# Step 0's second product by seven products on all rows, and step 1's outer convolution blocks by ScalarE taps and accumulating DMAs

## The chip, the core and the metric

The kernel runs on one core of a Trainium2 chip. The metric is device time in microseconds (us). Five engines work side by side, each through its own list of instructions in order: TensorE (PE, matmuls), VectorE (DVE), ScalarE (ACT), GpSimd (POOL) and SyncE (SP). SP and POOL issue DMAs, which sixteen DMA engines carry out; an engine whose next instruction waits for a semaphore holds everything behind it.

## The reference

```python
w = softmax(weight, axis=-1)                  # (8 heads, 7 taps)
x_pad = zeros of 6 rows ahead of x            # x: (8, 4096, 192) float32
out[b, s, h, g] = sum_k w[h, k] * x_pad[b, s + k, h, g]     # 24 columns to a head
h = out.reshape(32768, 192) @ w_in            # w_in: (192, 2048)
g = h / (1 + exp(-1.702 * h))                 # quick gelu
y = g @ w_out                                 # w_out: (2048, 192)
```

A causal convolution of seven taps along the sequence, one set of taps per head, then a two-layer network with the quick gelu between. All of it is float32; `w_in` and `w_out` arrive as 64-bit floats and are rounded to float32 in the kernel.

## The kernel before

The 32,768 tokens are taken in 32 steps (`big` from 0 to 31), each of 512 tokens from each half of the batch. A step has four parts. `transpose_x` (VectorE) turns the tokens of `xin` so that channels lie on partitions, into `xt`, in three blocks `c` of 64 channels by two. The convolution makes `conv_t` out of `xt`. The first product (`hidden`) makes `g`, the gelu of `conv_t` times `w_in_s`. The second (`second`) multiplies `g` by `w_out_s` and by sums of its blocks, the forms in `w_form`, and the result is turned back on VectorE (`turn`) and stored by SP (`store`).

From step 1 on both products use schemes with fewer block products than blocks, in return for sums of blocks. Step 0 differs, since the sums of the weights are not made yet: its first product is done plainly (`plain`), while VectorE and ScalarE round the weights piece by piece (`split`, `rounds`, `round_w_out`), and its second product, `second_first`, uses seven block products in place of eight (matrices in two by two blocks) on half of the 2048 rows of `w_out`, and plain products on the other half. In the code `first` and `other` are the two halves. A `go` of one step is three matmuls for 32 of 96 output columns each (`L802`) and one matmul of a list laid aside (`side`, `L808`), so that four 32-column matmuls fill the array. The lists have 45 such groups. Differences of blocks of `g` (`t1`, `t2`, and `b12`, `b21`, `b22` in place; 128x2048 each) and of `w_out` (`s1` to `s4`; 128x384 each) are made on VectorE in between.

While step 0's second product runs, four other things are prepared.

- **The convolution of step 1** (`prepare(1)`): for blocks 2, 0 and 1, the first tap on ScalarE (`L494`) and six `scalar_tensor_tensor` on VectorE (`L496`) into `conv_t`. Then `SUMS_C` on VectorE (`L391`, `L393`), and `cross`, DMAs on SP (`L532`) that copy `conv_t` over to the other half of the partitions, two short ones for `V1` and then the long ones.
- **The convolution of step 2** has block 1 on VectorE and blocks 0 and 2 as taps: `prepare_taps(2)` puts fourteen calls of `tap` into the list `ready`, and `next_tap` issues the next. A tap is a ScalarE multiplication (`L507`) into a scratch place (`tap_home`). For block 2 POOL adds it on (`L509`). For block 0 the seven taps are added by six accumulating DMAs of POOL's queue (`L521`) in the order of `TREE`: (1,2), (3,4), (5,6), (0,1), (3,5), (0,3). In the first steps the scratch places are rows of `g` (`first_taps`), which step 1's gelus overwrite later.
- **The forms** of `w_out`: `add_forms(stage)` copies on ScalarE (`L435`, `L433`) and adds by accumulating DMAs on POOL's queue (`L437`): 6, 7, 4 and 4 of them in stages 0 to 3. `end_forms` changes the sign of four forms on ScalarE (`L441`); it stands in `todo` behind step 2's preparation and so comes in step 1.
- **The sums of `w_in`** (`sums_w_in`), twenty on VectorE.

There is no scheduler: each engine's order is the order of the calls. What is to be done beside the matmuls is in the two lists: `work(us)` takes items off `todo` as long as their given cost fits into `us`, `need(label)` takes all up to a label. How the tap DMAs and the last forms stand to each other comes from these lines:

```python
        end_taps(2 if big < 3 and k == K - 1 else 0)     # in tap(), L503; end_taps(left) issues all but `left`
    ...
        second_first(between)                            # in first_step()
        add_forms(3)
        end_taps()
        load_x(3)
```

In `second_first`, `next_tap` is called seven times, for the seven taps of block 0; the last of them leaves two DMAs of the tree, which `end_taps()` issues behind the four of `add_forms(3)`.

In step 1, `hidden(1, 0, ...)` starts with products whose sums are taken out of the banks by ScalarE and VectorE, and with gelus out of `room` into `g` (`L629`) and out of the banks (`L625`); TensorE goes on to a bank when they have emptied it.

Of the kernel before, what the change touches and what calls it, by code (L numbers as in the profile page):

```python
# [15 lines left out]
def kernel(  # L16
# [29 lines left out]
    nc = tc.nc  # L46
# [7 lines left out]
    Q = 32  # L54
# [423 lines left out]
    taps = {c: [spot(i)[:, k : k + 2, :] for i in TAP_SPOTS[c] for k in (0, 2)] for c in TAP_SPOTS}  # L478
    first_taps = [row(0, k) for k in (6, 7, 10, 11, 14, 15)]

    def tap_home(big, c, k):
        if big < 3:
            return (first_taps if c == 0 else taps[3])[k - 1]
        return taps[c][k - 1]
# [18 lines left out]
    def tap(big, c, k):  # L503

        dst = own(big)[:, 2 * c : 2 * c + 2, :]
        home = tap_home(big, c, k) if k else dst
        act.mul(home, conv_src(big, c, k), cw[:, c, k : k + 1])  # L507
        if k and c not in DMA_TAPS:
            nc.gpsimd.tensor_add(dst, dst, home)  # L509
            return  # L510
        homes = [dst] + [tap_home(big, c, i) for i in range(1, K)]
        for a, b in TREE.get(k, ()):
            tree.append((homes[a], homes[b]))
        end_taps(2 if big < 3 and k == K - 1 else 0)

    tree = []

# [51 lines left out]
    def prepare(big):  # L569

        v1 = place(big, V1)
        def convs(*cs):
            times = act.mul if big == 1 else vec.tensor_scalar_mul
            for c in cs:
                for k in range(K):
                    yield "", 0.76 if k else 0.48, lambda c=c, k=k: conv(big, c, k, times=times)

        cost = 0.34 if big == 1 else 0.0
        yield from convs(2, 0) if big == 1 else convs(1)
        yield f"done {big}", 0.0, lambda: need(f"taps {big}")  # L580
        yield "", cost, lambda: sums_c(big, 0)
        yield f"first {big}", 0.0, lambda: cross_when(True, big, v1, v1 + 1)
        if big == 1:
            yield from convs(1)
        yield "", 0.0, lambda: cross_when(False, big, 0, C31)
        for i in range(1, len(SUMS_C)):
            yield "", cost, lambda i=i: sums_c(big, i)
        rest = (C31, V8) if big % 2 else (C31 + 1, NB)
        yield f"all {big}", 0.0, lambda: cross_when(False, big, *rest)
# [159 lines left out]
    def chunk_cols(c):  # L749
        return slice(c * Q, (c + 1) * Q)  # L750

    def second_first(fetch):

        n3, nk = NC * Q, 4
        first, other = (0, 2), (3, 1)

        def four(t, pi):
            return t.rearrange("p (v q h) e -> p v q h e", v=2, h=2)[:, :, pi, :, :]
# [7 lines left out]
            return pairs[:, :, pi // 2, n, :, pi % 2, :]  # L766

        ws = [w_out_s[:, m, :, :] for m in range(2)]
        a11, a12, a21, a22 = (four(t, pi) for t in ws for pi in first)
        b11, b12, b21, b22 = (rows4(n, pi) for pi in first for n in range(2))  # L770
        t1, t2 = (place4(flat_room[:, i * nk * TOK : (i + 1) * nk * TOK]) for i in range(2))
        w4 = nk * HD
        s1, s2 = (place4(w_form[:, i, :, :].rearrange("p k d -> p (k d)")) for i in (FORMS - 2, FORMS - 1))
        room0 = own(0)[:, V2:, :].rearrange("p b t -> p (b t)")
        s3, s4 = (place4(room0[:, i * w4 : (i + 1) * w4]) for i in range(2))
        p5, d21 = (flat_room[0:n3, (2 * nk + i) * TOK : (2 * nk + i + 1) * TOK] for i in range(2))
        p1, q12 = (room0[0:n3, 2 * w4 + i * TOK : 2 * w4 + (i + 1) * TOK] for i in range(2))
        assert 2 * w4 + 2 * TOK == (NB - V2) * T
        add, sub = vec.tensor_add, vec.tensor_sub
        js = slice(0, TOK // Q)  # L780

        c11, a, c12, c21 = (slots[i][h] for h in range(2) for i in range(2))
        side = []

        def listed(w, t):
            return [(w[:, v, h, :], t[:, v, :, h * T : (h + 1) * T]) for v in range(2) for h in range(2)]

        def plainly(m, n):
            return [p for pi in other for p in listed(four(ws[m], pi), rows4(n, pi))]

        def aside(banks, *stages):

            for steps, to, start, stop in stages:
                for c, bank in enumerate(banks):
                    for i, (w, t) in enumerate(steps):
                        last = i == len(steps) - 1
                        side.append((bank[n3:, :], w[:, chunk_cols(c)], t, start and i == 0, stop, last and chunk(to, c)))

        def go(bank, steps, first=True, more=False):
            for i, (w, t) in enumerate(steps):  # L800
                for c in range(NC):
                    nc.tensor.matmul(  # L802
                        chunk(bank, c), w[:, chunk_cols(c)], t,
                        start=first and i == 0, stop=not more and i == len(steps) - 1, skip_group_check=True,
                    )
                if side:
                    dst, w, t, start, stop, to = side.pop(0)
                    nc.tensor.matmul(dst, w, t, start=start, stop=stop and to is not False, skip_group_check=True)  # L808
                    if to is not False:
                        act.copy(to, dst)  # L810

        whole = lambda bank: bank[0:n3, :]
        rows11, rows12, rows22 = listed(a12, b21) + plainly(0, 0), plainly(0, 1), plainly(1, 1)
        cut = len(rows12) - 3
        aside((sums[0], sums[1], slots[2][0]), (plainly(1, 0), d21, True, True))
        aside((sums[0], sums[1], c12), (listed(s1, t1), p5, True, True), (rows12[cut:], q12, False, True))

        sub(t1, b12, b11)
        sub(t2, b22, t1)
        add(s1, a21, a22)  # L820
        sub(s2, s1, a11)
        go(a, listed(a11, b11))
        act.copy(p1, whole(a))
        go(c11, rows11[:8], more=True)
        add_forms(0)
        work(1.5)
        sub(b12, b22, b12)
        sub(s3, a11, a21)
        sub(s4, a12, s2)
        go(a, listed(s2, t2), first=False)  # L830
        act.copy(whole(c12), whole(a))
        go(c11, rows11[8:], first=False)
        add_forms(1)
        work(5.0)
        add(p1, p1, whole(c11))
        turn(0, 0, blocks(p1), js)
        sub(b21, b21, t2)
        go(a, listed(s3, b12), first=False)
        add(whole(c21), d21, whole(a))
        work(4.0)  # L840
        go(c12, listed(s4, b22) + rows12[:cut], first=False)
        add_forms(2)
        fetch()
        go(c21, listed(a22, b21), first=False)
        work(3.0)
        turn(1, 0, blocks(whole(c21)), js)
        store(0, 0)
        ready.extend(prepare_taps(2))
        next_tap()
        next_tap()  # L850
        for i in range(0, len(rows22), 2):
            go(a, rows22[i : i + 2], first=False)
            if i in (2, 4):
                act.copy(sums[i // 2 - 1], slots[2][i // 2 - 1])
            next_tap()
            if i < 2:
                next_tap()
        work(6.0)
        assert not side
        add(p5, p5, whole(a))  # L860
        add(q12, q12, whole(c12))
        turn(1, 1, blocks(p5), js)
        turn(0, 1, blocks(q12), js)
        store(0, 1)

# [198 lines left out]
    def first_step(fetch):  # L1064
# [84 lines left out]
        def stage_2():  # L1149
            round_w_out(0)  # L1150
            load_w_out(3)
            todo.append(("", 2.1, lambda: turn_x(1)))
            todo.extend(prepare(1))

        def last_stage():
            round_w_out(3)
            todo.extend(("", 0.42, lambda i=i: sums_w_in(i)) for i in range(len(SUMS_W)))
            todo.append(("sums", 0.0, lambda: None))

        split(3)  # L1160
        stages = [
            stage_0, stage_1, stage_2, lambda: split(6), lambda: round_w_out(1), None, None,
            lambda: split(7), None, lambda: round_w_out(2), None, last_stage,
        ]
        free = [slots[0], sums, slots[1], slots[2]]
        for u, m in ((0, 1), (1, 0), (1, 1)):
            for n in range(2):
                for v in range(2):
                    slot = free.pop(0)
                    free.append(slot)  # L1170
                    plain(u, m, n, v, slot)
                    gelu(2 * m + n, u, v, slot)
                    (stages.pop(0) or (lambda: work(2.3)))()
        give(False, 0)


        def between():
            need("all 1")
            for c in range(NC):
                transpose_x(2, c)  # L1180
            todo.extend(prepare(2))
            todo.append(("forms", 0.0, end_forms))
            fetch()

        second_first(between)
        add_forms(3)
        end_taps()
        load_x(3)
        need("sums")

    def turn_x(big):
        for c in range(NC):
# [61 lines left out]
```

## Time and profile before

| | |
|---|---|
| median of three runs | 2276.47 us (2276.09 to 2276.76) |
| the profiled execution | 2276.84 us |
| its span in the profile | 2274.8 us |
| granted TensorE clock, mean | 0.999 |
| step 0's first product ends, second product runs | 55.8 us, 55.8 to 95.7 us |
| TensorE busy from 80 to 100 us, from 120 to 140 us | 19.77 of 20 us, 19.49 of 20 us |
| VectorE, ScalarE, POOL busy from 80 to 100 us | 19.51, 12.00, 6.59 of 20 us |

How to read it: the page gives the busy time of each engine over the span, and the chain that ended last with its share by engine. The rows of instructions in order of time have start, duration, engine, line, operation, what is written and read, and how often. Times count from the span's start. A float32 matmul of the program makes two rows in the profile, the second pass right behind the first, and the ends of matmuls are modelled. `POOL ... DMA_DIRECT2D` is the time in which POOL issues a DMA; how long that takes to land stands in another view. In the rows by stretch the columns are the length, the busy time of PE, PEld, DVE, ACT and POOL with their counts, the granted clock, the busy share of the DMA engines and GB/s.

### The profile page before, as it was taken

Reading aid. Unit: us, or ns where it says so; the run is one execution under the profiler, and the core shown is the slowest. Engines: PE = TensorE matmul, PEld = TensorE weight load, DVE = VectorE, ACT = ScalarE, POOL = GpSimd, SP = SyncE. Lnnn points to the kernel's source line nnn. Section 1 sums busy time; section 2 is a strip of 40 time slices with the busy share of each in tenths; the row PEclk is TensorE's granted clock in tenths of the full one; section 3 lists DMA queues with packets and bytes.
Section 4 is the critical chain, followed back from the end, with each engine's and each line's share of the span. In section 5 each row is a group of like instructions: output and inputs, shape, how many; then the busy total and the mean of one; then the engine's idle time right before and its main releaser. Section 6 shows DMA issues by size and latency. Waiting matters only on the chain.

```text
span 2274.8 us, 60966 instructions
## 1 busy us (share of the span) xinstructions
PE 2266.5 (100%) x25238; PEld 1208.8 (53%) x25238; DVE 1944.9 (85%) x2795; ACT 1556.9 (68%) x2959; POOL 836.8 (37%) x825
## 2 busy tenths in 40 slices
PE   9999999999999999999999999999999999999999
PEld 5375555555555555555555555555555555555556
DVE  8898888888888888888888888888888888888877
ACT  7666776667766677666677666776667766667754
POOL 0444443244432443423444333443244442344400
PEclk9999999999999999999999999999999999999999
DMA  8866556766566665666656676656756566664443
GB/s 188 155 136 138 116 110 127 142 125 128 112 127 135 124 136 112 124 126 127 140 113 112 127 141 127 126 109 127 139 122 136 111 128 127 125 142 85 89 99 71
DMA packets 268932, 283.42 MB, mean 125 GB/s; under 512 B 117872, under 2 KB 205936, under 8 KB 268528
## 3 DMA queue, kind: packets, MB, share of 16 engines
q0 software_dynamic: 56352, 148.33, 36.3%
q1 hardware_dynamic: 210656, 130.80, 25.5%
q8 instruction: 199, 3.26, 0.6%
q14 instruction: 77, 0.63, 0.1%
q10 hardware_dynamic: 1648, 0.39, 0.1%
HBM read 53.15 MB, written 25.17 MB: 34 GB/s over the span
## 4 chain that ended last, share of the span: by engine, by line
PE 99%; ACT 0%; DVE 0%; DMA 0%; issue 0%; SPq 0%; DVEq 0%; ACTq 0%
PE slot L603 35%; PE slot L957 34%; PE sums L603 16%; PE sums L957 13%; PE slot L802 2%; DMA xin<-in_x_dram 0%; DVE xt L473 0%; ACT conv_t L1062 0%; DVE conv_t L496 0%; SPq L99 0%; ACT conv_t L357 0%; DVE room L644 0%; ACT conv_t L356 0%; DVE osbs L874 0%; ACT w_form L435 0%
## 5 line engine op out<-in xcount | busy, mean ns | idle before, releaser
L603 PE MATMUL slot<-conv_t,w_in_s 64*128 64x512 f32 x3740 | 861.1, 591 | 0.8 <-DVE room L644 0.5
L957 PE MATMUL slot<-g,w_form 128*32 128x256 f32 x7024 | 711.0, 379 | 0.0
L603 PEld LDWEIGHTS slot<-conv_t,w_in_s 64*128 64x128 f32 x3740 | 372.0, 187 | 429.9 <-issue 354.3
L393 DVE TENSOR_TENSOR g<-g 128x1024 f32<-128x1024 f32 x372 | 454.3, 1248 | 3.4 <-ACT g L629 0.2
L957 PEld LDWEIGHTS slot<-g,w_form 128*32 128x32 f32 x7024 | 376.3, 110 | 117.3 <-DVE room L644 0.5
L603 PE MATMUL sums<-conv_t,w_in_s 64*128 64x512 f32 x1660 | 407.5, 589 | 0.5 <-DVE w_in_s L376 0.3
L629 ACT ACTIVATE g<-room 128x1024 f32<-128x1024 f32 x310 | 326.2, 1079 | 68.3 <-DVE room L644 68.2
L982 ACT COPY room<-slot 32x256 f32<-32x256 f32 x434 | 159.0, 366 | 310.4 <-PE slot L957 309.3
L957 PE MATMUL sums<-g,w_form 128*32 128x256 f32 x2648 | 368.8, 379 | 0.0
L957 PE MATMUL slot<-g,w_out_s 128*32 128x256 f32 x4080 | 318.9, 380 | 0.0
L933 POOL DMA_DIRECT2D g<-g x124 | 106.3, 858 | 487.9 <-PE slot L957 155.4
L603 PEld LDWEIGHTS sums<-conv_t,w_in_s 64*128 64x128 f32 x1660 | 170.5, 187 | 187.8 <-issue 141.6
L509 POOL TENSOR_TENSOR conv_t<-conv_t,g 128x512 f32<-128x512 f32 x180 | 261.4, 1452 | 14.8 <-POOL conv_t L509 3.6
L521 POOL DMA_DIRECT2D g<-g x120 | 105.5, 882 | 435.2 <-PE sums L957 128.7
L640 ACT COPY room<-slot 128x512 f32<-128x512 f32 x434 | 231.8, 603 | 38.9 <-PE slot L603 38.9
L507 ACT ACTIVATE g<-xt,cw 128x512 f32<-128x512 f32 x360 | 248.7, 730 | 2.2
L957 PEld LDWEIGHTS slot<-g,w_out_s 128*32 128x32 f32 x4080 | 164.8, 110 | 128.8 <-ACT g L625 22.7
L625 ACT ACTIVATE g<-slot 128x512 f32<-128x512 f32 x334 | 180.8, 598 | 49.6 <-PE slot L603 29.5
L496 DVE SCALAR_TENSOR_TENSOR conv_t<-xt,cw,conv_t 128x512 f32<-128x512 f32 (+1 forms) x210 | 198.9, 947 | 10.6 <-ACT conv_t L494 5.9
L957 PEld LDWEIGHTS sums<-g,w_form 128*32 128x32 f32 x2648 | 178.2, 110 | 37.4
L393 POOL TENSOR_TENSOR conv_t<-conv_t 128x256 f32<-128x256 f32 x180 | 183.8, 1034 | 9.4
L982 ACT COPY room<-sums 32x256 f32<-32x256 f32 x217 | 79.3, 366 | 144.5 <-PE sums L957 142.8
(185 smaller groups left out, 2885.2 us busy)
## 6 DMA issues: line engine op xcount, KB each, us to landing
g<-g POOLq DMA_DIRECT2D x124, 512.0 KB, 5.6
xin<-in_x_dram SPq DMA_DIRECT2D x240, 180.0 KB, 4.4
conv_t<-conv_t SPq DMA_DIRECT2D x180, 192.0 KB, 3.2
g<-g POOLq DMA_DIRECT2D x120, 256.0 KB, 3.8
out_dram<-osbs SPq DMA_DIRECT2D x186, 128.0 KB, 4.9
g<-room POOLq DMA_DIRECT2D x31, 512.0 KB, 5.3
conv_t<-g POOLq DMA_DIRECT2D x60, 256.0 KB, 4.7
g<-osbs POOLq DMA_DIRECT2D x30, 512.0 KB, 4.7
```

The lines of the kernel that those rows point to most:

```text
L393: eng.tensor_sub(v(dst), v(a), v(b))
L496: vec.scalar_tensor_tensor(out=dst, in0=src, scalar=tap, in1=dst, op0=ALU.mult, op1=ALU.add)
L507: act.mul(home, conv_src(big, c, k), cw[:, c, k : k + 1])
L509: nc.gpsimd.tensor_add(dst, dst, home)
L521: nc.gpsimd.dma_start(out=out, in_=src, accum_op=ALU.add)
L603: nc.tensor.matmul(slot[h], w_in_s[halves[h], a, v * P : (v + 1) * P], src, start=first, stop=True, skip_group_check=True,)
L625: act.activation(dst[:, :, h, :], src[h].rearrange("p (o t) -> p o t", o=2), AF.Gelu_apprx_sigmoid)
L629: act.activation(dst.rearrange("p o h t -> p h o t"), src.rearrange("p h (o t) -> p h o t", o=2), AF.Gelu_apprx_sigmoid,)
L640: act.copy(bank(dst, h), bank(src, h))
L933: nc.gpsimd.dma_start(out=spot(dst), in_=spot(a), accum_op=ALU.add)
L957: nc.tensor.matmul(dst, w, t, start=first, stop=last, skip_group_check=True)
L982: act.copy(to, d)
```

## The change

Step 0's second product uses seven products for eight on both halves of the rows. `t1`, `t2` and `s1` to `s4` are made for both halves (`groups`), in places that are free by then: `places` in `w_in_s`, `osbs`, and blocks of `conv_t` of step 0. The lists have 42 groups of four matmuls. `second_first` is now a generator whose first three pieces (the first differences) run in the last stages of step 0's first product.

Step 1's convolution blocks 2 and 0 become taps: fourteen ScalarE multiplications, of which eleven are issued behind the gelus of the stages of step 0's first product and three by `last_taps`, and twelve accumulating DMAs on POOL's queue in the order of `TREE`, all of them before the first form. Their scratch places are `w_form` for block 2 and blocks of `conv_t` for block 0. Block 1 stays on VectorE, with its first tap there too. The order within `second_first` changes: the sums of `conv_t` and the crossings come before the middle of it (`need("conv 1")`, `need("first 1")`, `need("all 1")`), the turns and stores all at its end, and `next_tap` is called nine times.

```diff
+    flat_form = w_form.rearrange("p i f d -> p (i f d)")
+    homes_1 = {
+        2: [flat_form[:, i * TOK : (i + 1) * TOK].rearrange("p (o t) -> p o t", o=2) for i in range(3, 9)],
+        0: [conv_t[:, i, b : b + 2, :] for i in (1, 2) for b in (V2, V4, V6)],
+    }
     def tap_home(big, c, k):
+        if big == 1:
+            return homes_1[c][k - 1]
...
-        if k and c not in DMA_TAPS:
+        if k and c not in DMA_TAPS and big > 1:
             nc.gpsimd.tensor_add(dst, dst, home)
             return
...
-        end_taps(2 if big < 3 and k == K - 1 else 0)
+        end_taps(2 if big == 2 and k == K - 1 else 0)
...
-        yield from convs(2, 0) if big == 1 else convs(1)
+        yield from convs(1)
+        yield f"conv {big}", 0.0, lambda: None
...
-        go(a, listed(a11, b11))
-        act.copy(p1, whole(a))
-        go(c11, rows11[:8], more=True)
-        add_forms(0)
...
+        aside(
+            (sums[0], sums[1], c12),
+            (listed(s1, t1, (0,)), None, True), (listed(s1, t1, (1,)), p5, False), (p3[:6], q12, False),
+        )
+        last_taps()
+        sub(t1[1], b12[1], b11[1])
+        add(s1[1], a21[1], a22[1])
+        go(a, listed(a11, b11))
+        act.copy(p1, whole(a))
+        sub(t2[1], b22[1], t1[1])
+        for i in range(2):
+            sub(s2[i], s1[i], a11[i])
+        add_forms(0)
+        need("conv 1")
...
+        go(c11, p2[:6], more=True)
+        add_forms(1)
...
+        need("first 1")
...
+        need("all 1")
+        add(p1, p1, whole(c11))
+        go(a, listed(s3, b12), first=False)
+        add_forms(2)
+        between()
...
+        fetch()
+        for i in range(len(SUMS_W)):
+            sums_w_in(i)
+        next_tap()
+        next_tap()
+        steps = listed(a22, t2, (1, 0))
+        for i in range(0, len(steps), 2):
+            go(c21, steps[i : i + 2], first=False)
+            if i in (0, 2):
+                act.copy(sums[i // 2], slots[2][i // 2])
+            next_tap()
+            if i < 6:
+                next_tap()
...
+        taps_1 = [(c, k) for c in (2, 0) for k in range(K)]
+        def taps_next(n):
+            for _ in range(n):
+                tap(1, *taps_1.pop(0))
...
+        rest = second_first(between, fetch, lambda: taps_next(len(taps_1)))
+        def stage(n, todo=lambda: next(rest)):
+            todo()
+            taps_next(n)
...
+            stage_0, stage_1, stage_2, lambda: split(6), stage_4, lambda: stage(1, lambda: split(7)),
+            lambda: stage(2, lambda: round_w_out(2)), lambda: stage(2, lambda: round_w_out(3)),
+            lambda: stage(2), lambda: stage(2), lambda: stage(1), lambda: stage(1, lambda: work(1.3)),
...
-        second_first(between)
+        for _ in rest:
+            pass
         add_forms(3)
         end_taps()
         load_x(3)
```

More of the change, by code (lines that the diff above doesn't have):

```diff
@@ L572, in convs @@
         def convs(*cs):
-            times = act.mul if big == 1 else vec.tensor_scalar_mul
             for c in cs:
                 for k in range(K):
-                    yield "", 0.76 if k else 0.48, lambda c=c, k=k: conv(big, c, k, times=times)
+                    yield "", 0.76 if k else 0.48, lambda c=c, k=k: conv(big, c, k)
         cost = 0.34 if big == 1 else 0.0
-        yield from convs(2, 0) if big == 1 else convs(1)
+        yield from convs(1)
+        yield f"conv {big}", 0.0, lambda: None
         yield f"done {big}", 0.0, lambda: need(f"taps {big}")
@@ L582, in prepare @@
         yield f"first {big}", 0.0, lambda: cross_when(True, big, v1, v1 + 1)
-        if big == 1:
-            yield from convs(1)
         yield "", 0.0, lambda: cross_when(False, big, 0, C31)
@@ L750, in chunk_cols, with second_first @@
         return slice(c * Q, (c + 1) * Q)
-    def second_first(fetch):
-        n3, nk = NC * Q, 4
-        first, other = (0, 2), (3, 1)
+    def second_first(between, fetch, last_taps):
+        n3 = NC * Q
+        groups = ((0, 2), (3, 1))
         def four(t, pi):
@@ L768, in second_first @@
         ws = [w_out_s[:, m, :, :] for m in range(2)]
[L769 to L773, printed above, removed]
-        room0 = own(0)[:, V2:, :].rearrange("p b t -> p (b t)")
[L775 to L778, printed above, removed]
+        a11, a12, a21, a22 = ([four(t, pi[j]) for pi in groups] for t in ws for j in range(2))
+        b11, b12, b21, b22 = ([rows4(n, pi[j]) for pi in groups] for j in range(2) for n in range(2))
+        w4, t4 = NG * HD, NG * TOK
+        room0 = own(0)[:, V2:, :].rearrange("p b t -> p (b t)")
+        old0 = own(0)[:, 0:V2, :].rearrange("p b t -> p (b t)")
+        t1 = [place4(flat_room[:, 0:t4]), place4(places[:, 0:t4])]
+        t2 = [place4(flat_room[:, t4 : 2 * t4]), place4(osbs)]
+        s1, s2, s3, s4 = (
+            [place4(flat[:, i * w4 : (i + 1) * w4]) for flat, i in two]
+            for two in (
+                ((flat_form, FORMS - 2), (old0, 0)), ((flat_form, FORMS - 1), (old0, 1)),
+                ((room0, 0), (old0, 2)), ((room0, 1), (room0, 2)),
+            )
+        )
+        p5, q12 = (flat_room[0:n3, 2 * t4 + i * TOK : 2 * t4 + (i + 1) * TOK] for i in range(2))
+        p1 = room0[0:n3, 3 * w4 : 3 * w4 + TOK]
+        assert 3 * w4 + TOK <= (NB - V2) * T and 3 * w4 <= V2 * T
         add, sub = vec.tensor_add, vec.tensor_sub
@@ L783, in second_first, with listed @@
         side = []
[L785 to L789, printed above, removed]
+        def listed(w, t, gs=(0, 1)):
+            return [
+                (w[i][:, v, h, :], t[i][:, v, :, h * T : (h + 1) * T])
+                for i in gs for v in range(2) for h in range(2)
+            ]
         def aside(banks, *stages):
-            for steps, to, start, stop in stages:
+            for steps, to, start in stages:
                 for c, bank in enumerate(banks):
                     for i, (w, t) in enumerate(steps):
-                        last = i == len(steps) - 1
-                        side.append((bank[n3:, :], w[:, chunk_cols(c)], t, start and i == 0, stop, last and chunk(to, c)))
+                        last = to is not None and i == len(steps) - 1
+                        side.append((bank[n3:, :], w[:, chunk_cols(c)], t, start and i == 0, last and chunk(to, c)))
         def go(bank, steps, first=True, more=False):
@@ L805, in go @@
                     )
[L806 to L810, printed above, removed]
-        whole = lambda bank: bank[0:n3, :]
-        rows11, rows12, rows22 = listed(a12, b21) + plainly(0, 0), plainly(0, 1), plainly(1, 1)
-        cut = len(rows12) - 3
-        aside((sums[0], sums[1], slots[2][0]), (plainly(1, 0), d21, True, True))
@@ L816, in second_first, with sums_b @@
[L816 to L821, printed above, removed]
+                dst, w, t, start, to = side.pop(0)
+                nc.tensor.matmul(dst, w, t, start=start, stop=to is not False, skip_group_check=True)
+                if to is not False:
+                    act.copy(to, dst)
+        whole = lambda bank: bank[0:n3, :]
+        def sums_b(i):
+            sub(b12[i], b22[i], b12[i])
@@ L822, in second_first @@
+        sub(t1[0], b12[0], b11[0])
+        yield
+        sub(t2[0], b22[0], t1[0])
+        yield
+        add(s1[0], a21[0], a22[0])
+        work(1.3)
+        yield
+        p2, p3 = listed(a12, b21), listed(s4, b22)
+        aside(
+            (sums[0], sums[1], c12),
+            (listed(s1, t1, (0,)), None, True), (listed(s1, t1, (1,)), p5, False), (p3[:6], q12, False),
+        )
+        last_taps()
+        sub(t1[1], b12[1], b11[1])
+        add(s1[1], a21[1], a22[1])
         go(a, listed(a11, b11))
@@ L823, in second_first @@
         act.copy(p1, whole(a))
-        go(c11, rows11[:8], more=True)
+        sub(t2[1], b22[1], t1[1])
+        for i in range(2):
+            sub(s2[i], s1[i], a11[i])
         add_forms(0)
[L826 to L829, printed above, removed]
+        need("conv 1")
+        for i in range(2):
+            sub(s4[i], a12[i], s2[i])
+            sub(s3[i], a11[i], a21[i])
+        go(c11, p2[:6], more=True)
+        add_forms(1)
+        sums_b(0)
@@ L830, in second_first @@
+        sums_b(1)
         go(a, listed(s2, t2), first=False)
         act.copy(whole(c12), whole(a))
-        go(c11, rows11[8:], first=False)
-        add_forms(1)
-        work(5.0)
-        add(p1, p1, whole(c11))
-        turn(0, 0, blocks(p1), js)
[L837 to L844, printed above, removed]
@@ L845, in second_first @@
-        work(3.0)
+        go(c11, p2[6:], first=False)
+        need("first 1")
+        sub(t2[0], b21[0], t2[0])
+        sub(t2[1], b21[1], t2[1])
+        need("all 1")
+        add(p1, p1, whole(c11))
+        go(a, listed(s3, b12), first=False)
+        add_forms(2)
+        between()
+        act.copy(whole(c21), whole(a))
+        add(p5, p5, whole(a))
+        go(c12, p3[6:], first=False)
+        fetch()
+        for i in range(len(SUMS_W)):
+            sums_w_in(i)
+        next_tap()
@@ L846, in second_first @@
+        next_tap()
[7 more added lines that the diff above has]
+                next_tap()
+        assert not side
+        turn(0, 0, blocks(p1), js)
+        turn(1, 1, blocks(p5), js)
+        add(q12, q12, whole(c12))
         turn(1, 0, blocks(whole(c21)), js)
         store(0, 0)
-        ready.extend(prepare_taps(2))
@@ L849, in second_first @@
[L849 to L862, printed above, removed]
         turn(0, 1, blocks(q12), js)
@@ L1151, in stage_2, with stage_4, between @@
             load_w_out(3)
-            todo.append(("", 2.1, lambda: turn_x(1)))
+        def stage_4():
+            round_w_out(1)
+            turn_x(1)
             todo.extend(prepare(1))
[L1155 to L1158, printed above, removed]
+        taps_1 = [(c, k) for c in (2, 0) for k in range(K)]
+        def taps_next(n):
+            for _ in range(n):
+                tap(1, *taps_1.pop(0))
+        def between():
+            for c in range(NC):
+                transpose_x(2, c)
+            todo.extend(prepare(2))
+            todo.append(("forms", 0.0, end_forms))
+            ready.extend(prepare_taps(2))
+        rest = second_first(between, fetch, lambda: taps_next(len(taps_1)))
+        def stage(n, todo=lambda: next(rest)):
+            todo()
+            taps_next(n)
         split(3)
         stages = [
-            stage_0, stage_1, stage_2, lambda: split(6), lambda: round_w_out(1), None, None,
-            lambda: split(7), None, lambda: round_w_out(2), None, last_stage,
+            stage_0, stage_1, stage_2, lambda: split(6), stage_4, lambda: stage(1, lambda: split(7)),
+            lambda: stage(2, lambda: round_w_out(2)), lambda: stage(2, lambda: round_w_out(3)),
+            lambda: stage(2), lambda: stage(2), lambda: stage(1), lambda: stage(1, lambda: work(1.3)),
         ]
@@ L1172, in first_step @@
                     gelu(2 * m + n, u, v, slot)
-                    (stages.pop(0) or (lambda: work(2.3)))()
+                    stages.pop(0)()
         give(False, 0)
[L1177 to L1183, printed above, removed]
-        second_first(between)
+        for _ in rest:
+            pass
         add_forms(3)
@@ L1188, in first_step @@
         load_x(3)
-        need("sums")
     def turn_x(big):
```

## The prediction

> **What bounds the kernel now.** I read the page first, then the instructions in order of time around step 0's second product (56 to 96 us) and step 1 (96 to 140 us), engine by engine, then the DMA view of single stretches for the times to landing.
>
> ```profile
> PE 2266.5 (100%) x25238; PEld 1208.8 (53%) x25238; DVE 1944.9 (85%) x2795; ACT 1556.9 (68%) x2959; POOL 836.8 (37%) x825
> PE 99%; ACT 0%; DVE 0%; DMA 0%; issue 0%; SPq 0%; DVEq 0%; ACTq 0%
> q0 software_dynamic: 56352, 148.33, 36.3%
> q1 hardware_dynamic: 210656, 130.80, 25.5%
> ```
>
> TensorE is the bound and the whole chain. A matmul less is time less; a TensorE wait that is new anywhere is time more, and later steps have no idle time to win it back. Queue 0 holds POOL's accumulating DMAs: 148.33 MB in 36.3% of 2274.8 us, or 180 GB/s, so 256 KB cost 1.46 us of all sixteen engines and 192 KB 1.09 us at best. Queue 1 (SP's) does 225 GB/s.
>
> ```profile
> 55.77 0.63 PE L802 MATMUL slot<-g,w_out_s 128*32 128x512 f32 x3
> 56.22 0.61 PE L802 MATMUL slot<-g,w_out_s 128*32 128x512 f32 x3
> 95.73 1.13 PE L603 MATMUL slot<-conv_t,w_in_s 64*128 64x512 f32 x4
> ...
> 64.25 5.44 POOL L437 DMA_DIRECT2D w_form<-w_out_s  x6 [60.17 <-DVE w_form L820]
> 71.78 4.39 POOL L437 DMA_DIRECT2D w_form<-w_out_s  x5 [0.32 <-ACT w_form L435]
> 83.96 1.86 POOL L437 DMA_DIRECT2D w_form<-w_form  x2 [6.03 <-DMA w_form<-w_form]
> 98.22 1.70 POOL L521 DMA_DIRECT2D conv_t<-g  x1
> 100.04 3.44 POOL L437 DMA_DIRECT2D w_out_s<-w_form  x2
> 115.18 1.19 POOL L521 DMA_DIRECT2D conv_t<-g  x1 [10.46 <-DMA g<-g]
> ...
> 111.90 1.16 ACT L629 ACTIVATE g<-room 128x1024 f32<-128x1024 f32 x1
> 115.75 1.88 ACT L441 ACTIVATE w_form<-w_form 128x384 f32<-128x384 f32 x4
> ```
>
> Start and end of the second product, then POOL's queue, then two ScalarE instructions that depend on it: the gelu at 111.90 overwrites rows of `g` in which step 2's channel-0 taps lie, so it needs the tree DMA issued at 98.22; the sign changes at 115.75 need the last forms, issued at 100.04. Neither waited.
>
> ```profile
> conv_t<-g POOLq DMA_DIRECT2D x1, 256.0 KB, 6.5
> w_out_s<-w_form POOLq DMA_DIRECT2D x2, 192.0 KB, 11.9
> w_form<-w_form POOLq DMA_DIRECT2D x2, 192.0 KB, 6.4
> 64.00:84.00 20.00, 20.00 (x192) 5.94 (x184) 16.91 (x24) 9.24 (x20) 13.40 (x16) 1.00 0.98 156
> q0 software_dynamic: 2223, 2.37, 53.8%
> ```
>
> Times to landing of those DMAs (6.5 us: landed 104.7; the forms about 113), then 64 to 84 us, where the DMA engines are 0.98 busy at 156 GB/s, and queue 0's share of them from 91 to 120 us: the DMA engines are full for 50 us, and the two waits have 7.2 and 4 us of slack.
>
> **The change, part by part.** (1) Matmuls. The second product goes from 45 groups (three `L802`, one `L808`) to 42. The first and last rows above give (95.73 - 55.77 - 1.1 for the four `L603` between) / 45 = 0.86 us for a group: **-2.6 us**.
>
> (2) ScalarE gains 14 tap multiplications at 0.63 us (two `L507` start to end take 1.33 us) and loses three `L494`. Eleven taps (7.0 us) stand behind the gelus of step 0's first product, where ScalarE now idles 5.5 us between 41 and 56 us (five gaps, each for TensorE) and two `L494` go (1.4 us): just enough, but a gelu can stand behind two taps. The last gelu on the bank that the second product opens with ends at 54.4 us today, 1.4 us before TensorE needs it. So 0 to 2 us, nearest to the taps' own 0.63 us a piece: **+0.9**. The last tap ends near 61 us, since the final gelu pair is at 55.9 to 56.9 and three taps stand behind it.
>
> (3) VectorE. Differences over 128x2048 go from four to eight (+4 x 2.28 us), those over 128x384 from four to eight (+4 x 0.48), and twelve `L496` at 0.77 us and their waits on ScalarE (2.71 us before 74.62, 1.71 before 55.01) go: +2 us of work against 4 us of waits. I take 0; without that cover its last sums of `w_in_s` come up to 2 us late and hold step 1's first matmuls. Sides in the bank that ScalarE has just filled wait for a 0.56 us copy and the end of a matmul: **+0.9**, at one place.
>
> (4) POOL's queue. Twelve accumulations of 256 KB now stand ahead of the 17 forms. Each tree ends in two dependent ones, and POOL holds everything behind one that waits. Alone, one takes 3.8 us to land (the page's median). From the last tap at 61, two waits of some 5 us follow, so the first form is issued near **72 instead of 64.25 us**. Fifteen forms at 192 KB / 156 GB/s = 1.26 us land from 75 to 92.7. SP's four long copies of `conv_t` (1.57 MB, 7.0 us at 225 GB/s), today mostly behind the forms (`L532`, from 83 us), now fall among them: 99.7. The last two wait for others to land: 6.4 us, so 106.
>
> Step 2's first four tree DMAs (5.9 us of engine time) come next, beside six output stores and eight loads of `x` (2.2 MB) on SP. With 53.8% of the engines they take 10.9 us: the one that the gelu needs lands at 117, not 104.7. The bounds are 112 (no sharing) and 122 (forms as late as 109 and even sharing of small packets). The gelu is due at 111.9 - 1.4 (the two `L507` before it are now done earlier) - 0.8 (the sum so far, -2.6 + 0.9 + 0.9) = 109.7. ScalarE waits 7.3 us (2 to 12); TensorE has 1.0 us in hand there (it goes on to the bank of the next gelu pair, which ends at 114.0, at 115.0): **+6.3** (1 to 11).
>
> (5) The last four forms. Today POOL issues them ahead of the two last tree DMAs of step 2. The new `second_first` calls `next_tap` nine times, not seven; the eighth is channel 2's first tap, whose `end_taps(0)` flushes those two ahead of the forms. The second of them waits for the first four's end. Counted from the landing at 117: 1.5 us for the next, 0.5 issue, 1.85 for a `L509` addition in between (11.11 us / 6), 3.1 to the first form, 3 x 1.2 to the last: 10.5 us. ScalarE comes to the fourth sign change 5.1 us after the gelu (111.9 to 117.0). So it waits a second time, 5.4 us; of this 0.3 us take the place of today's small gap at 118: **+5.1**. If (4) had no wait, this would still stand, less the slack: 1 to 7.
>
> Sum: -2.6 + 0.9 + 0.9 + 6.3 + 5.1 = **+10.6 us**. Against the profiled execution's own 2276.84 us that is 2287.4, and since that execution lies 0.4 us over the median of 2276.47, **2287 us** for the median.
>
> By the Trainium skill (TensorE: Matmul & The Clock Gate, Part 1) a TensorE idle for some 3.4 us falls to half clock and runs so for as long again. No row here has such an idle time later than the start, where the first ten 128x128 matmuls took 2.50 us, over twice the 0.11 us apiece that 0.43 us for 512 columns gives. By that rule each of the two waits would cost 1.7 us more, and the sum would be +12 to +14.
>
> **Rivals.** (A) *The DMAs keep up*: not slower. If the chain on queue 0 ends 7 us earlier, both waits vanish and -2.6 + 1.8 = -0.8 is left: 2276. It decides at a landing before 110 us. For it: the forms issued at 64 ran without SP beside them, and taps are in larger pieces than forms. Against it: the engines were already 0.98 busy from 64 to 84 and the change adds 12 x 1.46 = 17.5 us of work to that stretch. By the rows' 180 GB/s it has a small chance: 0.12. The Trainium skill (DMA: Bandwidth & Descriptors, Anatomy of one DMA) fits POOL's DMAs with 436 GB/s beyond a fixed 2 us, an estimate of 0.6 us for 256 KB, by which this rival would win at 2276; the 1.46 us of the rows disagree. (B) *Only the order of the forms bites*: the first wait is hidden, the second costs 5.1: +4.3, 2281, a chance of 0.10. (C) *Deeper backlog*: sharing as bad as at 100 to 113 us today (four forms of 0.79 MB took over 8 us, twice their 1.1 us each), or a cold TensorE after the waits: +16 to +22, near 2295, 0.20. (D) *Faster*: all of today's small waits between 84 and 132 us vanish too (0.7 us that the waits view shows, 1.9 us of VectorE at 129.4) and nothing new appears: -5.2, 2271, 0.02.
>
> **How the numbers follow.** The forecast (+6 to +16) has 0.56, A 0.12, B 0.10, C 0.20, D 0.02. The range 2278.5 to 2297 leaves out A, D and the end of C. About 0.2% (4.6 us) is what a measurement of this kernel can tell from no change. Slower by more holds for the forecast, C and half of B: 0.82. Within it: A, half of B: 0.16. Faster: D, 0.02.
>
> **What would show it.** The page would show TensorE idle some 15 us more than now, in two pieces between 110 and 135 us in front of step 1's matmuls, released by ScalarE; a ScalarE gelu there waiting on a DMA of `conv_t<-g`, and the fourth sign change on a form. The first form's issue near 72 us, the last of the seventeen landing near 106. The second product in 42 groups over 36 us. It is wrong if the gelu meets its DMA landed (A), or if TensorE waits on VectorE at the start of step 1 instead.

## The result, and the profile after

The changed kernel takes **2293.23 us** (median of six runs, 2292.4 to 2294.15) against 2276.61 us for the kernel before beside it: a ratio of **1.0073, 95% interval 1.006 to 1.0086**, 16.6 us slower. The profiled execution took 2293.8 us, 17.0 more than that of before, with a span of 2292.1 us.

The page of the changed kernel, first the busy time by engine, then the two queues and the chain that ended last:

```profile
PE 2271.0 (99%) x25214; PEld 1203.4 (53%) x25214; DVE 1935.3 (84%) x2791; ACT 1563.6 (68%) x2968; POOL 844.4 (37%) x837
...
q0 software_dynamic: 58080, 151.48, 36.8%
q1 hardware_dynamic: 210656, 130.80, 25.3%
...
PE 94%; DMA 4%; DVE 1%; POOL 1%; SPq 0%; issue 0%; ACT 0%; POOLq 0%; ACTq 0%; DVEq 0%
```

The chain was 99% TensorE before; now 4% of it are DMAs. TensorE has 24 matmul rows fewer and yet 4.5 us *more* busy time: a busy TensorE can be a slow one. The rows of TensorE from the end of the second product on, in order of time, show both where it stood still and where it was slow:

```profile
94.14 1.13 PE L609 MATMUL slot<-conv_t,w_in_s 64*128 64x512 f32 x4
98.93 2.08 PE L609 MATMUL sums<-conv_t,w_in_s 64*128 64x512 f32 x4 [3.66 <-DMA conv_t<-conv_t]
100.77 2.57 PE L609 MATMUL slot<-conv_t,w_in_s 64*128 64x512 f32 x8
103.16 1.04 PE L609 MATMUL sums<-conv_t,w_in_s 64*128 64x512 f32 x4
...
121.67 5.88 PE L609 MATMUL slot<-conv_t,w_in_s 64*128 64x512 f32 x16 [3.74 <-ACT g L631]
133.36 2.56 PE L609 MATMUL slot<-conv_t,w_in_s 64*128 64x512 f32 x4 [5.80 <-ACT room L646]
135.22 4.11 PE L609 MATMUL sums<-conv_t,w_in_s 64*128 64x512 f32 x8
```

Three waits of 3.7, 3.7 and 5.8 us, each in brackets with what released it. Four rows of 64x512 take about 1.1 us at 94 and 103 us, but 2.1 and 2.6 right behind the first and the third wait. The rows by stretch give the reason (length, PE, PEld, DVE, ACT and POOL busy with their counts, granted clock, DMA share, GB/s):

```profile
95.30:98.90 3.60, 0.00 (x0) 0.00 (x0) 3.60 (x7) 2.04 (x4) 0.00 (x0) 0.97 1.02 170
98.90:102.30 3.40, 3.37 (x8) 1.65 (x10) 0.81 (x2) 1.79 (x4) 0.00 (x0) 0.53 0.99 161
...
121.60:126.00 4.40, 4.33 (x11) 2.44 (x13) 1.91 (x1) 3.69 (x8) 2.79 (x4) 0.61 0.30 44
...
133.30:140.00 6.70, 6.64 (x16) 5.44 (x18) 3.86 (x4) 3.51 (x7) 6.39 (x5) 0.53 0.09 21
```

The granted clock is 0.53 to 0.61 behind each wait. Counted between the starts of the matmuls, less their usual distance, the three waits cost 3.8, 3.9 and 6.4 us, and the half-rate matmuls behind them 1.7, 1.9 and 3.2 us.

What the waits end on stands on POOL's queue and on ScalarE:

```profile
74.00 0.86 POOL L529 DMA_DIRECT2D conv_t<-conv_t  x1 [3.42 <-DMA conv_t<-conv_t]
74.54 5.62 POOL L437 DMA_DIRECT2D w_form<-w_out_s  x6
...
103.16 0.86 POOL L437 DMA_DIRECT2D w_form<-w_form  x1 [11.75 <-DMA w_form<-w_form]
105.06 0.86 POOL L437 DMA_DIRECT2D w_form<-w_form  x1 [1.04 <-DVE slot L650]
105.96 3.64 POOL L529 DMA_DIRECT2D g<-g  x3
112.47 1.19 POOL L529 DMA_DIRECT2D conv_t<-g  x1 [2.88 <-DMA g<-g]
...
123.21 1.19 POOL L529 DMA_DIRECT2D conv_t<-g  x1 [4.74 <-PE slot L609]
...
125.18 2.28 POOL L437 DMA_DIRECT2D w_form<-w_out_s  x2
126.33 2.90 POOL L437 DMA_DIRECT2D w_out_s<-w_form  x2
...
120.08 1.06 ACT L635 ACTIVATE g<-room 128x1024 f32<-128x1024 f32 x1 [5.91 <-DVE room L650]
...
132.31 0.52 ACT L441 ACTIVATE w_form<-w_form 128x384 f32<-128x384 f32 x1 [7.01 <-DMA w_out_s<-w_form]
```

The first form is issued at 74.54 (64.25 before), the last of the seventeen at 105.06, step 2's tap DMAs behind them, the last four forms from 125.18 on (98.95 before). The row puts the gelu at 120.08 down to VectorE, but the sum it reads was ready at 115 us; the DMA issued at 112.47 lands at 120.0. The view of DMA issues for single stretches (KB each, median us from issue to landing) gives that and the first wait's DMA, two DMAs of 512 KB of SP's long crossing, issued at 85.1 and 85.6 (median 7.4 us before). They took 10.2 and 13.2 us; the second landed at 98.8, where the first wait ends. The third line is for the two forms issued at 89.67, on whose landing POOL then stands for 11.75 us:

```profile
conv_t<-conv_t SPq DMA_DIRECT2D x2, 512.0 KB, 11.7
...
conv_t<-g POOLq DMA_DIRECT2D x1, 256.0 KB, 7.5
...
w_form<-w_form POOLq DMA_DIRECT2D x2, 192.0 KB, 13.7
```

### The profile page after: what moved, and what is told of

Same layout as the page of the kernel before. It is cut to its first block, busy times and chain, and to the rows that moved or that the text cites. A ratio compares the mean times of both kernels' runs of the same rounds, so it can differ in the third digit from the quotient of the medians.

```text
span 2292.1 us, 60960 instructions
## 1 busy us (share of the span) xinstructions
PE 2271.0 (99%) x25214; PEld 1203.4 (53%) x25214; DVE 1935.3 (84%) x2791; ACT 1563.6 (68%) x2968; POOL 844.4 (37%) x837
## 4 chain that ended last, share of the span: by engine, by line
PE 94%; DMA 4%; DVE 1%; POOL 1%; SPq 0%; issue 0%; ACT 0%; POOLq 0%; ACTq 0%; DVEq 0%
PE slot L609 33%; PE slot L986 33%; PE sums L609 15%; PE sums L986 12%; DMA w_form<-w_form 1%; DMA g<-g 1%; DMA g<-in_moe_w_in_dram 1%; DMA conv_t<-conv_t 0%; POOL w_form L437 0%; SPq L296 0%; DMA osbs<-in_moe_w_out_dram 0%; DMA w_out_s<-w_form 0%; SPq L99 0%; ACT w_form L515 0%; POOL conv_t L529 0%
## 5 line engine op out<-in xcount | busy, mean ns | idle before, releaser
L609 PE MATMUL slot<-conv_t,w_in_s 64*128 64x512 f32 x3740 | 862.3, 593 | 9.8 <-ACT room L646 5.8
L609 PEld LDWEIGHTS slot<-conv_t,w_in_s 64*128 64x128 f32 x3740 | 374.8, 188 | 439.6 <-issue 354.3
L609 PE MATMUL sums<-conv_t,w_in_s 64*128 64x512 f32 x1660 | 407.3, 593 | 3.9 <-DMA conv_t<-conv_t 3.7
L609 PEld LDWEIGHTS sums<-conv_t,w_in_s 64*128 64x128 f32 x1660 | 170.9, 188 | 191.7 <-issue 142.0
L504 DVE SCALAR_TENSOR_TENSOR conv_t<-xt,cw,conv_t 128x512 f32<-128x512 f32 (+1 forms) x198 | 185.6, 938 | 4.6
```

The costliest lines, as they stand in the source:

```text
L504: vec.scalar_tensor_tensor(out=dst, in0=src, scalar=tap, in1=dst, op0=ALU.mult, op1=ALU.add)
L609: nc.tensor.matmul(slot[h], w_in_s[halves[h], a, v * P : (v + 1) * P], src, start=first, stop=True, skip_group_check=True,)
```

## The experiments

The theory: TensorE loses its time by waiting for what stands on a queue that twelve more accumulating DMAs have made late, and by the lower clock behind each wait. All times below are medians, with the ratio to the kernel before on the same chip, which took 2276.5 to 2276.7 us each time.

**The order of the last DMAs alone undone.**

```diff
-        end_taps(2 if big == 2 and k == K - 1 else 0)
+        end_taps(2 if big == 2 and k in (0, K - 1) else 0)
```

> The changed kernel, with the two last tree DMAs of step 2 kept back until the last four forms are issued, as before the change. Theory (the order on POOL's queue makes the third wait of TensorE, 6.4 us at 133 us, and the half-rate matmuls behind it, 3.2 us): both go, the two earlier waits stay, 2293.2 - 9.6 = 2284 us (2282 to 2287). Rival (the forms are late because the DMA engines are full, whatever the order): the third wait shrinks by less than 2 us, 2291 to 2293 us.

2287.03 us, ratio 1.0045 (1.0033 to 1.0058). TensorE's waits:

```profile
PE slot L609 <- ACT g L631: 5.3, 1, 5.3
PE sums L609 <- DMA w_form<-w_out_s: 3.4, 1, 3.4
```

The second line is the first wait, which the view puts down to a form; the second of the two long DMAs landed at 98.35 and TensorE went on at 98.48. The third wait is gone, so the order made it. The gain is 6.2 us, not 9.6: the DMA for the gelu landed at 121.2 here, so the second wait is 1.6 us longer, and a gap of 0.9 us came at 141 us.

**Half of the tap DMAs by GpSimd's own additions.**

```diff
-        if k and c not in DMA_TAPS and big > 1:
+        if k and c not in DMA_TAPS:
```

> The changed kernel, with the six additions of step 1's block 2 by GpSimd itself in place of six accumulating DMAs (8.8 us of the DMA engines' time at 1.46 us each). Theory (the three waits end when the chain on POOL's queue ends, so what makes the chain shorter moves all three): the first form is issued near 66 us in place of 74.5, the long crossing lands before 96 us, the DMA that the gelu needs before 115 us; the third wait stays, but ends 5 to 8 us earlier: 2285 to 2288 us. Rival (the waits come from the order of the instructions, not from the load): 2292 us or more. Other rival: GpSimd's additions are slower than the DMAs they replace and step 1's sums come later still: over 2295 us.

2290.3 us, ratio 1.006 (1.0048 to 1.0073): between theory and rivals, and for a reason in none of them. The first form came at 71.9, not 66, and TensorE had a new wait of 5.0 us near 62 us, for VectorE; of the three waits only the third was left (5.4 us). POOL's and VectorE's rows in this run:

```profile
47.98 11.28 POOL L517 TENSOR_TENSOR conv_t<-conv_t,w_form 128x512 f32<-128x512 f32 x6 [43.90 <-ACT w_form L515]
...
49.23 5.63 DVE L376 SCALAR_TENSOR_TENSOR w_out_s<-w_form 128x96 f32<-128x96 f32 x8
54.78 3.35 DVE L829 TENSOR_TENSOR room<-g 128x2048 f32<-128x2048 f32 x1
58.24 3.17 DVE L831 TENSOR_TENSOR room<-g,room 128x2048 f32<-128x2048 f32 x1
```

and VectorE's in the changed kernel, where POOL adds nothing there:

```profile
49.28 1.44 DVE L376 SCALAR_TENSOR_TENSOR w_out_s<-w_form 128x96 f32<-128x96 f32 x8
50.63 2.29 DVE L829 TENSOR_TENSOR room<-g 128x2048 f32<-128x2048 f32 x1
53.03 2.29 DVE L831 TENSOR_TENSOR room<-g,room 128x2048 f32<-128x2048 f32 x1
```

The same VectorE instructions take 12.2 us in place of 6.0 while POOL adds. Since TensorE comes later for this reason, the run says nothing clean of the queue's length.

**Each part alone.** First the products, with step 1's convolution back on VectorE and no taps for it:

```diff
+        if big == 1:
+            yield from convs(2, 0)
         yield from convs(1)
...
-        taps_1 = [(c, k) for c in (2, 0) for k in range(K)]
+        taps_1 = []
```

> One part of the change alone: seven products on all rows with its places and its order of the work, but step 1's blocks 2 and 0 on VectorE as before. Theory (only the DMAs of the taps cost time): the first form is issued near 64 us, no wait for a DMA is over 1 us; VectorE has 12 x 0.77 = 9.3 us more, of which the 4.5 us that it now waits for the taps give a part; TensorE waits for VectorE by the rest: 2276.6 - 2.6 + 4.8 = 2279 us, up to 2284 with half-rate matmuls behind the wait. Rival (the rearranged product itself brings the loss): 2290 us or more.

2283.37 us, ratio 1.003 (1.0019 to 1.0041). TensorE's waits:

```profile
PE slot L817 <- DVE g L829: 3.4, 1, 3.4
PE slot L611 <- ACT room L648: 2.1, 1, 2.1
```

The forms start at 64.0 and VectorE is late, as expected; half-rate matmuls follow both waits. Not expected was the second wait: the fourth sign change waits 2.1 us for a form, since the order of the last DMAs is the new one. Then the taps alone, in the kernel before, with the scratch places and the stages that they have in the changed one, and the sums of `conv_t` where it has them:

```diff
-        yield from convs(2, 0) if big == 1 else convs(1)
+        yield from convs(1)
+        yield f"conv {big}", 99.0 if big == 1 else 0.0, lambda: None
...
+                tap(1, *taps_1.pop(0))
...
-        work(5.0)
+        need("conv 1")
+        work(5.0)
```

> The other part alone: the kernel before, with its 45 groups and its order, and step 1's blocks 2 and 0 by ScalarE taps and accumulating DMAs ahead of the forms. Theory: the backlog on the queue is the same; the gelu, due at 111.9 us, waits for a DMA that lands near 120 us, TensorE loses 7 us there and 1.7 us by half-rate matmuls; the last four forms stand in the old order, so no third wait: 2285 us (2281 to 2289). Rival (the taps cost nothing by themselves, the loss needs the new product's order): 2277 us or less.

2288.89 us, ratio 1.0053 (1.004 to 1.0065). The gelu's DMA lands at 120.4 and TensorE waits 5.6 us for it, as expected; 2.0 us more are a wait that was not, for step 2's crossing at 142 us, and another 1.3 us a wait for VectorE at 87 us:

```profile
PE slot L609 <- ACT g L631: 5.6, 1, 5.6
PE slot L609 <- DMA conv_t<-conv_t: 2.0, 1, 2.0
```

So the taps bring 12 us without the new product. The two parts together give 16.6 us, less than 6.7 + 12.2: with the taps, TensorE no longer waits for VectorE.

**Half of the taps, and the order.** Block 0 of step 1 goes back to VectorE and block 2 stays with the DMAs, with the order of the first experiment:

```diff
+        if big == 1:
+            yield from convs(0)
         yield from convs(1)
...
-        taps_1 = [(c, k) for c in (2, 0) for k in range(K)]
+        taps_1 = [(c, k) for c in (2,) for k in range(K)]
```

> The changed kernel with two edits: step 1's block 0 back on VectorE (six of the twelve accumulating DMAs, 8.8 us of the DMA engines' time, and seven ScalarE taps go; 0.48 + 6 x 0.77 us of VectorE come back), and the two last tree DMAs of step 2 behind the last four forms. Theory (the queue's length is the price; VectorE has room for one block in the time in which it now waits 4.5 us for the taps): first form near 65 us, the long crossing lands by 95, the gelu's DMA by 114; what is left of the waits is under 2 us: 2276.6 - 2.6 + 2 = 2276 us (2273 to 2279). Rival (VectorE is the bound as soon as a block comes back, as with both: 6.7 us over the kernel before): 2280 us or more.

**2274.87 us, ratio 0.9992 (0.9983 to 1.0001)**: all three waits are gone. The chain is short again (first form at 63.96, the gelu's DMA lands at 100.2) and TensorE is not interrupted:

```profile
100.00:120.00 20.00, 20.00 (x96) 11.53 (x94) 14.93 (x21) 18.89 (x34) 10.89 (x10) 1.00 1.03 176
```

This is 18 us better than the changed kernel and 1.6 us better than the kernel before, but the interval reaches just past 1, so the latter is not told from no change. With the same edit and the new order left as it is:

> Step 1's block 0 back on VectorE as in the run before that did both edits, and this edit alone: the two last tree DMAs of step 2 stay ahead of the last four forms. Theory (with half of the tap DMAs gone the queue has run empty by then): the gelu's DMA lands near 100 us, the forms by 112, ahead of the sign changes at 117: 2275 to 2277 us, the order no longer matters. Rival (the order costs what it costs, whatever the load; it was 6.2 us with all twelve tap DMAs): 2279 us or more.

2278.0 us, ratio 1.0007 (0.9998 to 1.0016): 1 us over the theory's times and 1 us under the rival's. The gelu's DMA landed at 100.5 as expected, but the last four forms landed up to 118.0, not 112:

```profile
105.14 1.19 POOL L529 DMA_DIRECT2D conv_t<-g  x1 [4.80 <-DMA g<-g]
...
107.10 2.27 POOL L437 DMA_DIRECT2D w_form<-w_out_s  x2
...
118.06 0.52 ACT L441 ACTIVATE w_form<-w_form 128x384 f32<-128x384 f32 x1 [1.75 <-DMA w_out_s<-w_form]
```

POOL stood 4.8 us for the tree even with six tap DMAs fewer, and the DMA engines were still full (busy share 1.02 from 98 to 106 us). Between the medians the order costs 3.1 us here and 6.2 us with all the taps.

**The lower clock by itself.** Matmuls that nobody reads fill TensorE's waits, 26 ahead of the third in one run, 15 and 9 ahead of the first two in another:

```diff
+    def fill(to, n):
+        for _ in range(n):
+            nc.tensor.matmul(to[:, 0:P], w_in_s[:, 6, 0:P], w_in_s[:, 6, 0:P], start=True, stop=True)
...
+        if v and big == 1:
+            fill(bank(y, 0), 26)
         pe(sums, 0)
```

> The changed kernel with 26 matmuls of 128x128 (0.21 us each, 5.5 us) that nobody reads, into a free bank, ahead of the matmul that waits third (133.4 us). They fit into the wait. Theory (TensorE falls to half rate by having been idle): the 3.2 us of half-rate matmuls behind the third wait go, the wait's end stays where the form lands: 2293.2 - 3.2 = 2290 us. Rival (those matmuls are slow for another reason, such as the order of their banks or full DMA engines): 2293 us.

> The same with 15 such matmuls ahead of the first wait and 9 ahead of the second (3.2 and 1.9 us). The half-rate matmuls behind them (1.65 and 1.9 us) go. Theory (the second and the third wait end at the landing of a DMA, whenever TensorE comes): what is won is waited for again, the third wait grows by some 3 us, 2293 us. Rival (the three waits and their half-rate stretches add up as they stand): 2293.2 - 3.5 = 2289.7 us.

2290.23 us, ratio 1.006 (1.0048 to 1.0073), and 2291.75 us, ratio 1.0068 (1.0055 to 1.008). With the third wait filled the run is 3.0 us shorter than the changed kernel, as the first theory has it; the intervals of the two ratios overlap, but the clock leaves no doubt, whole behind the filled wait where it was 0.53:

```profile
133.90:137.00 3.10, 3.10 (x15) 1.48 (x16) 2.62 (x3) 2.33 (x4) 2.94 (x3) 1.00 0.00 0
```

In the other run the clock is whole behind the first wait, and low behind the third, which has grown by 1.5 us (from 5.8 to 7.3 us idle):

```profile
98.60:102.00 3.40, 3.40 (x17) 1.66 (x17) 1.13 (x3) 2.01 (x5) 0.00 (x0) 1.00 1.00 170
...
132.80:137.00 4.20, 4.11 (x10) 3.46 (x12) 2.63 (x3) 3.51 (x7) 4.04 (x3) 0.53 0.00 0
```

TensorE came to the third wait 2.0 us earlier than in the changed kernel, but the wait ended only 0.5 us earlier (132.89 for 133.36): a wait that ends at a DMA's landing swallows most of what is won ahead of it. The time of 2291.75 us lies between the theory (2293) and the rival (2289.7), and its interval excludes neither, so this rests on the trace of one execution.

**Without the forms' additions.**

```diff
-        for dst, src in SUMS_O[stage]:
+        for dst, src in ():
```

> The changed kernel without the 21 accumulating DMAs that add up the forms (their copies on ScalarE stay), so the sums of w_out's blocks are left out of the computation. Theory (the taps are no trouble by themselves, the forms behind them are the backlog): queue 0 is empty by 78 us, the long crossing lands by 94 and the gelu's DMA by 105; no wait over 1 us is left: 2276.6 - 2.6 = 2274 us (2272 to 2277). Rival (the crossings are late because VectorE waits 4.5 us for the end of the tap tree): the first wait stays with over 2 us: 2277 us or more.

2274.32 us, ratio 0.999 (0.9981 to 0.9999). No wait of TensorE is left, the crossing lands 5.3 us after its issue, and VectorE waits for the tap tree as long as in the changed kernel (4.5 us there):

```profile
conv_t<-conv_t SPq DMA_DIRECT2D x2, 512.0 KB, 5.3
...
DVE conv_t L393 <- DMA conv_t<-conv_t: 4.6, 1, 4.6
```

So the rival (the first wait comes from VectorE's lateness) falls: the forms beside the crossing make it late. The run also shows what the change can bring with this order when nothing is late, some 2 us.

**Full engines, or a queue that stands.** All taps stay, but VectorE adds the last six forms, among them the two in front of which POOL stood (11.75 us in the row at 103.16):

```diff
-        [(19, 17), (20, 18), (21, 19), (22, 20)],
-        [(23, 0), (24, 3), (1, 22), (7, 21)],
+        [(19, 17), (20, 18)],
+        [(21, 19), (22, 20), (23, 0), (24, 3), (1, 22), (7, 21)],
...
+            if stage == 3:
+                vec.tensor_add(form(dst), form(dst), form(src))
```

> The changed kernel with all twelve tap DMAs, but the last six forms (the two that POOL waits for, and the last four) are added by VectorE (0.48 us each) where the last four were issued. Theory (the second wait comes from POOL standing in front of two waiting forms from 85 to 105 us, with step 2's taps behind them): step 2's taps are issued from 95 us on, the gelu's DMA lands before 112; the second and the third wait go, the first stays (3.8 us and 1.7 us at half rate), VectorE comes some 2 us late to its first sums of step 1: 2276.6 - 2.6 + 0.9 + 5.5 + 2 = 2282 us (2279 to 2285). Rival (the DMA engines are full until 118 us, so the gelu's DMA lands as late as ever): 2287 us or more.

2282.05 us, ratio 1.0025 (1.0015 to 1.0034), the time that was expected: step 2's taps are issued from 91.2 us on, the gelu's DMA is issued at 104.60 and lands at 111.7, and of the three waits the first is left, beside one for VectorE:

```profile
91.19 1.41 POOL L532 DMA_DIRECT2D g<-g  x1
...
104.60 1.19 POOL L532 DMA_DIRECT2D conv_t<-g  x1 [5.46 <-PE sums L612]
...
PE sums L612 <- DMA conv_t<-conv_t: 2.9, 1, 2.9
PE slot L612 <- DVE slot L653: 1.9, 1, 1.9
```

The parts differ from the expected ones: the first wait is 2.9 us, not 3.8, with no half rate behind it, and the matmuls at half rate (1.7 us) follow the wait for VectorE instead. That the sum came out is in part luck. The DMA engines are as full as ever (share 1.1 from 80 to 120 us). So 8 of the 15 us by which the gelu's DMA was late are gone when POOL does not stand in front of two waiting forms; the transfers of these two, which are gone as well, can be 2 x 1.1 us of that, so the standing is 6 to 8 us. What POOL stood for was itself made long by full engines: the forms that it waited on took 13.7 us to land in the changed kernel.

## Why the prediction was right or wrong

The direction, the two forecast waits and their causes were right; the time came out 6 us above the forecast, just past the end of its case (+16) and at the beginning of rival C (a deeper backlog, or a cold TensorE after the waits). It was both. That the time still lies in the stated range is owed to the part of C that the range takes in.

- **(1) 42 groups for 45, -2.6 us: right.** From 55.86 to 94.14 us, less 1.1 us for `L609` between and the 0.9 us of (3), is 36.3 us, or 0.86 us a group. The run without the forms' additions nets -2.2.
- **(2) Taps before the gelu, +0.9: wrong, 0.1.** The second product starts at 55.86 in place of 55.77.
- **(3) VectorE 0, a copied bank +0.9: right.** Two passes of three matmuls (74.77 and 75.20 us) run without their fourth, which waits for the bank that ScalarE copies from 75.05 to 75.61; the two left over run alone at 85.13 and 85.56, 2 x 0.43 us. TensorE does not wait for VectorE in the changed kernel. With both blocks back on it, VectorE costs 3.4 us of waiting and half-rate matmuls behind, so the taps do buy something, only for more than it is worth.
- **(4) The backlog: right in kind, too short.** First form 74.54 for 72 (the tap tree made POOL wait three times, not twice), the last of the seventeen landed at 110 for 106, the gelu's DMA at 120.0 for 117. Not foreseen was that SP's long crossing would itself be late (11.7 us to landing) and stop TensorE 20 us earlier, at 95 to 98.9. For the second wait the forecast was TensorE +6.3; the first and the second wait cost 3.8 + 3.9 and 3.6 at half rate, 11.3. The prediction had both full engines and POOL's standing in one chain; the run with the forms on VectorE parts them, 6 to 8 of the 15 us for the standing.
- **(5) The order of the last four forms: right in kind, +5.1 forecast, 6.4 measured**, with 3.2 us at half rate behind it; undoing that order wins 6.2 us.
- **Clock.** The prediction left it out of its sum and gave it 1.7 us a wait in a sentence by itself. It was there at all three: 1.7, 1.9 and 3.2 us.

The sum by the trace: -2.6 + 0.1 + 0.9 (these three give the 1.6 us by which the second product ends earlier) + 14.1 (three waits) + 6.8 (half rate) - 2.3 (small gaps of before between 95 and 132 us that the waits swallowed; this last term is what is left over) = +17.0; the two profiled executions differ by 17.0. The terms that were too small are those of (4) and (5): they were taken as what two waits add, at full clock. What counts is where the chain ends: the fourth sign change came at 132.3, where the prediction's own steps give 127.5 (117 + 10.5), 4.8 us late, and 3.2 us at half rate follow. The first wait, which is in no term, changed the time little, since the later waits take up most of what is lost ahead of them. The chances are off by a hundredth: by the stated split, slower is 0.81 and within 0.17.

Rivals A (the DMAs keep up) and B (only the order bites) did not happen with twelve more DMAs on the queue. With six and the old order of the last DMAs, what A describes did: 2274.87 us, where A was priced at 2276. With six and the new order it was what B describes, at a lower price: 2278.0 us for 2281.

## What to carry to other kernels

Before work is moved onto a DMA queue that is already full, follow the queue to its last entry, and ask which entry waits for a landing and what is queued behind it: an in-order queue that stands is as late as one that is full. Try moving half: here six accumulating DMAs cost nothing measurable in either order of the last DMAs, and twelve cost 10.3 us in the old order and 16.6 in the new. Waits that end on a landing don't simply add up, and a wait of some microseconds of TensorE should be priced with the half-rate matmuls behind it.

## What the runs showed of the hardware

- **Half clock behind shorter waits than 3.4 us, and not behind all.** The Trainium skill (TensorE: Matmul & The Clock Gate, Part 1) has a window of some 3.4 us that runs freely and must pass idle. The waits of 3.7 us and more agree. But in the run with the forms on VectorE a wait of 2.9 us left the clock whole and one of 1.9 us, 9 us later, did not:

```profile
95.00:98.00 3.00, 0.13 (x4) 0.07 (x2) 2.97 (x7) 2.13 (x5) 0.04 (x1) 1.00 1.04 180
98.00:102.00 4.00, 4.00 (x19) 2.09 (x21) 1.00 (x2) 2.66 (x6) 1.14 (x1) 1.00 1.17 188
104.00:106.00 2.00, 0.69 (x3) 0.00 (x0) 1.96 (x5) 1.69 (x4) 1.19 (x1) 1.00 1.16 173
106.00:110.00 4.00, 3.42 (x8) 2.55 (x10) 2.97 (x5) 1.31 (x3) 0.70 (x1) 0.57 1.05 176
```

  A window that runs freely fits it that the length of a wait alone does not decide; a need of 3.4 us idle does not fit the 1.9. The waits of 2.1 and 2.0 us in the runs with the products alone and with one block back in the new order were followed by half-rate matmuls as well; one of 2.1 us in the run that fills the first two waits was not. What decides is open.
- **VectorE beside POOL's additions.** Eight `scalar_tensor_tensor` of 128x96 took 5.63 us in place of 1.44, two sums of 128x2048 6.5 in place of 4.6. The Trainium skill (SBUF — State Buffer, SBUF: two separate sides) tells of a port pair that VectorE with two inputs from SBUF and GpSimd take from one another for a whole instruction; these rows agree in direction. The first 4.2 us more are a little over two POOL additions of 1.88 us. That the port is the cause is not shown.
- **Landing times under load.** The same crossing took 5.3 us (median of its two DMAs of 512 KB) with no forms beside it, 7.4 before and 11.7 in the changed kernel; the DMA engines' busy share from 80 to 100 us was 0.72, 0.96 and 1.09.
